# One PSUM pool of double banks for everything, longer score runs, and the first k loaded in three parts

## The chip, the cores and the metric

The kernel runs on one core of a Trainium2 chip. The metric is device time in microseconds (us) of that core. A span in a profile is counted from the first to the last instruction and is about 1.7 us shorter than the device time of the same run. Engines: PE is TensorE, PEld its weight loads, ACT is ScalarE, DVE is VectorE, POOL is GpSimd, SP is SyncE.

## The reference

Block-sparse attention (4 batches, 8 heads, 768 tokens, head size 64), then a two-layer network with a gated first layer. All in fp32.

```python
scores = q @ k.T / 8                       # 768 x 768 for each of 32 heads
scores = where(mask, scores, -1e9)         # window, first and last blocks, 3 random blocks a row
attn   = softmax(scores) @ v
x   = attn reordered to [3072 tokens, 512]
h   = x @ w_in                             # [3072, 2048]
g   = h * sigmoid(beta * h)
out = g @ w_out                            # [3072, 512]
```

## The kernel before

The kernel has a planner of its own. It describes all work as nodes with a planned duration and buffers, `order_of` puts the nodes in an order for each engine, and the instructions are emitted in that order. The buffers come from pools; the planner gives a buffer to a node when the slot is free by its own clock. The semaphore waits of the program come from the tiles that the instructions read and write, not from the planner.

PSUM holds two kinds of tiles: two double tiles of two banks each for scores (`sc`), four single banks for everything else (`mm`).

```python
SLOTS = {"st_k": 3, "st_q": 6, "st_v": 4, ..., "et": 15, "xst": 7, ..., "osb": 2,
         "sc": 2, "mm": 4}
...
T = {
    "sc": many(psum, "sc", [P, 2, 512], FP32),
    "mm": many(psum, "mm", [P, 512], FP32),
    ...
}
def at(buf):
    return T[buf.pool][buf.slot]
```

A score step fills one double tile (for two heads: 128 keys by 512 queries, or 256 by 256), and one exponential reads it whole:

```python
def mm(sc=sc, kc0=kc0):                       # "sc": 64 rows, the rest of PE's work has 128
    for i in range(kn):
        for hh in range(2):
            nc.tensor.matmul(at(sc)[:, hh, i * n:(i + 1) * n], lhsT=kX[...], rhs=qX[...],
                             start=True, stop=True)
def ex(eng, sc=sc, et=et):
    nc.scalar.activation(out=at(et)..., in_=at(sc)..., func=AF.Exp, bias=0.0, scale=SCALE)
```

The first layer makes 16 groups (`hp`) for each block of tokens; a tanh (`th`) on ACT and a gate multiply (`gm`) on DVE both read the group's bank. After them come the second-layer groups (`op`), whose bank is copied out to `osb`.

```python
for f in range(N_FFC):                        # 16
    hb, tb = Buf("mm"), Buf("t_sb")
    def hp(f=f, hb=hb):
        for c in range(NPAIR):                # 4
            nc.tensor.matmul(at(hb)[:, 0:n], lhsT=w_in_sb[:, c, f * P:(f + 1) * P],
                             rhs=xT_sb[:, c, t0:t0 + n], start=(c == 0), stop=(c == NPAIR - 1))
    def th(eng, f=f, hb=hb, tb=tb):
        nc.scalar.activation(out=at(tb)[:, 0:n], in_=at(hb)[:, 0:n], func=AF.Tanh,
                             bias=0.0, scale=beta_h_sb[:, f:f + 1])
    def gm(eng, f=f, hb=hb, tb=tb):
        nc.vector.scalar_tensor_tensor(out=at(gb)[:, f, 0:n], in0=at(tb)[:, 0:n], scalar=1.0,
                                       in1=at(hb)[:, 0:n], op0=ALU.add, op1=ALU.mult)
```

The rest of PE's work: transposes (`turn`, `xt`), attention times v (`av`, normalized by a reciprocal `rc` and a multiply `nm` on DVE). There are two token blocks of 256 (the first and the last) and five of 512.

The softmax here doesn't subtract the row's maximum and nothing guards it: scores larger than these inputs give would overflow.

Of the kernel before, what the change touches and what calls it, by code (L numbers as in the profile page):

```python
# [23 lines left out]
class Node:  # L24


    def __init__(self, kind, eng, dur, lat, emit, deps=(), take=(), use=(), moved=0,
# [10 lines left out]
        self.start = self.done = self.on = None  # L38


BIAS = {"av": 39, "beta": 625, "cast": 183, "dma": -860, "ex": 395, "gm": -151, "hp": 34,
        "load": 1245, "lone sc": 160, "mask": -541, "mk": 266, "next sc": -48, "norm": 134,
        "op": 45, "op on": 85, "osb": 304, "sc": -79, "spread": 28, "th": 302, "turn": -1220,
        "turn cp": 47, "weights": 444, "x cp": 29, "x turn": -13}

W_GATE = (3, "k")
SLACK = 1500.0
AHEAD = 3
HOP = 60.0
SWITCH = 100.0  # L50
RATE = {"SP": 305.0, "POOL": 410.0}
# [2 lines left out]
SHARED = 42.0  # L54


def order_of(nodes, free, slots):

    free = dict(free)
    give = {p: [(0.0, s) for s in range(n)] for p, n in slots.items()}  # L60
    rows = 128
    wire = {"SP": 0.0, "POOL": 0.0}
    port = {"DVE": 0.0, "POOL": 0.0}
    left, after, at_dep = {}, {}, {}
    todo = []
    for n in nodes:
        left[n] = len(n.deps)
        at_dep[n] = n.at
        for d, x in n.deps:
            after.setdefault(d, []).append((n, x))  # L70
        if not n.deps:
            todo.append(n)
    out = []
    while todo:
        best = None
        for n in todo:
            ready = at_dep[n]
            want = {}
            for b in n.take:
                want[b.pool] = want.get(b.pool, 0) + 1  # L80
            ok = True
            for p, c in want.items():
                if len(give[p]) < c:
                    ok = False
                    break
                ready = max(ready, sorted(give[p])[c - 1][0])
            if not ok:
                continue
            for e in n.eng:
                n_start = max(ready, free[e])  # L90
                if n.port and e in port:
                    n_start = max(n_start, port["POOL" if e == "DVE" else "DVE"])
                bias = BIAS[n.kind]
                if n.rows == 64:
                    if rows == 64:
                        bias += BIAS["next sc"]
                    elif sum(t <= n_start for t, _ in give["sc"]) < 2:
                        bias += BIAS["lone sc"]
                key = (n_start + n.dur[e] - min(n.dur.values()) + bias, n.place)
                if best is None or key < best[0]:  # L100
                    best = (key, n, e, n_start)
        if best is None:
            raise RuntimeError("no node can start")
        _, n, e, start = best
        if e == "PE" and n.rows != rows:
            start, rows = start + SWITCH, n.rows
        n.on, n.start = e, start
        free[e] = start + n.dur[e]
        if n.port and e in port:
            port[e] = free[e]  # L110
        if n.moved:
            other = "POOL" if e == "SP" else "SP"
            t, rest, rate = max(wire[e], start + DMA_FIRST[e]), n.moved, RATE[e]
            if e == "SP" and wire[other] > t:
                both = min(rest, (wire[other] - t) * SHARED)
                wire[other] += both / RATE[other]
                t, rest = t + both / SHARED, rest - both
            wire[e] = t + rest / rate
            n.done = wire[e] + DMA_LAST
        else:  # L120
            n.done = free[e] + n.tail
        for b in n.take:
            t, b.slot = min(give[b.pool])
            give[b.pool].remove((t, b.slot))
        for b in n.use:
            b.users -= 1
            b.end = max(b.end, n.done)
            if b.users == 0:
                give[b.pool].append((b.end + HOP, b.slot))
        todo.remove(n)  # L130
        out.append(n)
        for m, x in after.get(n, ()):
            at_dep[m] = max(at_dep[m], n.done + HOP + x)
            left[m] -= 1
            if left[m] == 0:
                todo.append(m)
    if len(out) < len(nodes):
        raise RuntimeError("some nodes never become ready")
    return out
# [3 lines left out]
def kernel(  # L143
# [16 lines left out]
    P = 128  # L160
# [9 lines left out]
    VW = D + 2  # L170
    Q1 = 256

    SLOTS = {"st_k": 3, "st_q": 6, "st_v": 4, "s16_k": 4, "s16_q": 2, "set": 4, "va": 5,
             "et": 15, "xst": 7, "recip": 6, "t_sb": 5, "g": 2, "osb": 2, "sc": 2, "mm": 4}

    persist = ctx.enter_context(tc.tile_pool(name="persist", bufs=1))
    psum = ctx.enter_context(tc.tile_pool(name="psum", bufs=1, space=bass.MemoryType.PSUM))
# [1 line left out]
    def many(pool, tag, shape, dtype):  # L179
        return [pool.tile(shape, dtype, name=f"{tag}_{i}") for i in range(SLOTS[tag])]  # L180

    T = {
        "sc": many(psum, "sc", [P, 2, 512], FP32),
        "mm": many(psum, "mm", [P, 512], FP32),
        "et": many(persist, "et", [P, 2, 512], FP16),
        "xst": many(persist, "xst", [P, 4, 2, D], FP16),
        "recip": many(persist, "recip", [P, 2, 2, 1], FP32),
# [10 lines left out]
        T[f"s16_{nm}"] = many(persist, f"s16_{nm}", [P, 2 * NC * D], FP16)  # L198

    def at(buf):  # L200
        return T[buf.pool][buf.slot]

    identity = persist.tile([P, P], FP16, name="identity")
# [157 lines left out]
    def by_chunk(s16, lo, hi):  # L361
        return at(s16)[:, lo * P:hi * P].rearrange("p (c h d) -> p h c d", h=2, d=D)

    def add_load(nm, x, st, lo, hi, gate):
        b, j = pairs[x]
        src = {"k": k, "q": q, "v": v}[nm]

        def load():
            hg = src[b, 2 * j:2 * j + 2].rearrange("h (g p c) d -> p (h g) (c d)", g=NG, p=P)
            o = at(st).rearrange("p h (g c) -> p (h g) c", g=NG)  # L370
            if hi - lo == NC:
                nc.sync.dma_start(out=o, in_=hg)
            else:
                for g in range(lo // CG, hi // CG):
                    nc.sync.dma_start(out=o[:, g::NG], in_=hg[:, g::NG])
        deps = [(d, -1e9) for d in last_load + begin]
        kw = {"take": [st]}
        if gate is not None:
            def shut():
                nc.gpsimd.tensor_copy(out=at(st)[0:1, 0, lo * D:lo * D + 1],  # L380
                                      in_=w_out_sb[0:1, gate * 8, 0:1])
            deps.append(add("weights", "POOL", 600, 50, shut, deps=[w_out_of[gate]], take=[st]))
            kw = {"use": [st]}
        last_load[:] = [add("load", "SP", 500 if hi - lo in (NC, CG) else 1000, 0, load, deps=deps,
                             moved=68000 * (hi - lo) + (500000 if x == 0 and nm == "v" else 0),
                             **kw)]
        return last_load[0]

    def add_cast(x, nm, st, dst, lo, hi, load):
        w = (hi - lo) * P  # L390

        def cast(eng):
            e = nc.vector.tensor_copy if eng == "DVE" else nc.gpsimd.tensor_copy
            src = at(st)[:, :, lo * D:hi * D].rearrange("p h (c d) -> p h c d", d=D)
            e(out=at(dst)[:, :, :, 0:D] if nm == "v" else by_chunk(dst, lo, hi),  # L395
              in_=src)
        return add("cast", ("DVE", "POOL"), {"DVE": 60 + 0.53 * w, "POOL": 50 + 0.94 * w}, 90, cast,
                   deps=[(load, SLACK if x >= NPAIR else 4000 if lo and x == 3 else 0)],
                   take=[dst], use=[st], port=True)

    def add_half(x, nm, kq, lo, hi, first, gate):

        i = "kq".index(nm)
        w = (hi - lo) * P
        st, s16 = Buf(f"st_{nm}"), Buf(f"s16_{nm}")
        load = add_load(nm, x, st, lo, hi, gate)
        if x < NPAIR and lo == 0:
            loads[x, nm] = st, load
        c = add_cast(x, nm, st, s16, lo, hi, load)
        if x >= N_PE_TURN:  # L410
            def turn():
                nc.sync.dma_start_transpose(
# [18 lines left out]
    def add_prep(x, gates=(None, None, None)):  # L431
        kq, va, st = Buf("set"), Buf("va"), Buf("st_v")
        hi = Q1 // P if x < NPAIR else NC
        tk = add_half(x, "k", kq, 0, NC, None, gates[0])
        tq = add_half(x, "q", kq, 0, hi, tk, gates[1])
        lv = add_load("v", x, st, 0, NC, gates[2])
        cv = add_cast(x, "v", st, va, 0, NC, lv)
        prep[x] = {"kq": kq, "va": va, "k": tk, "q": tq, "q on": tq, "v": cv}
        if x < NPAIR:
            loads[x, "v"] = st, lv  # L440

# [6 lines left out]
    def tile_steps(x, q0, n):  # L448
# [5 lines left out]
        for kc0 in range(0, NC, kn):  # L454
# [19 lines left out]
            def mk(eng, et=et, kc0=kc0):  # L474
# [3 lines left out]
                    [P, 2 * CG * kn, w])  # L478
                nc.vector.tensor_tensor(out=e, in0=e, in1=m, op=ALU.mult)  # L479

            steps.append((x, q0, sc, et, mm, ex, mk,
                          [mask_of[g] for g in range(q0 // (CG * P), (q0 + n) // (CG * P))]))
        return steps, ets

    sc_of = {}

    def add_step(step, unit):
        x, q0, sc, et, mm, ex, mk, masks = step
        r = prep[x]
        g = add("sc", "PE", 218, 180, mm, deps=[(r["k"], SLACK if x >= N_PE_TURN else 0),  # L490
                      (r["q"] if q0 == 0 else r["q on"], SLACK if x >= N_PE_TURN else 0)],
                take=[sc], use=[r["kq"]], rows=64)
        sc_of.setdefault(unit, g)
# [197 lines left out]
```

## Time and profile before

| | before |
|---|---|
| device time, median of 3 runs | 280.38 us (280.29 to 280.6) |
| profiled span | 280.1 us |
| busy share PE / ACT / DVE | 95% / 76% / 75% |
| the chain that ended last | 83% PE |

The profiled execution is one of its own, at 281.79 us. Its PE clock was 0.74 of full speed between 20 and 33 us and full before and after that up to 62 us.

From the page of the kernel before: its first part (busy us, share of the span), two rows of the 40 slices, the chain, and four groups of instructions (busy us, mean ns of one, idle time before them and what ended most of it):

```profile
PE 265.3 (95%) x2455; PEld 139.5 (50%) x2455; DVE 209.5 (75%) x424; ACT 212.9 (76%) x281; POOL 28.0 (10%) x45
...
PE   4597899999999999999999999999999999999994
...
PE 83%; ACT 7%; DVE 4%; DMA 3%; issue 2%; SPq 0%; ACTq 0%; DVEq 0%
...
L591 PE MATMUL mm<-w_out_sb,g 128*128 128x512 f16 x384 | 93.3, 380 | 0.0
L567 PE MATMUL mm<-xT_sb,w_in_sb 128*128 128x512 f16 (+1 forms) x448 | 89.9, 349 | 0.4
L576 DVE SCALAR_TENSOR_TENSOR g<-t_sb,mm 128x512 f16<-128x512 f16 (+1 forms) x112 | 66.0, 608 | 23.3 <-ACT t_sb L572 22.2
L572 ACT ACTIVATE t_sb<-mm,beta_h_sb 128x512 f16<-128x512 f32 (+1 forms) x112 | 67.8, 649 | 12.9 <-PE mm L567 12.1
```

L567 is the first layer, L591 the second; PE waits for nothing ahead of them (0.4 and 0.0 us in all). After the first eighth of the span PE is full, so in that part time falls only if PE gets less to do, and rises with any wait put in front of PE.

What the two readers of a bank do during a run of first-layer groups shows in the timeline of before at 231 us (start, duration, engine, instruction, number merged, idle before and releaser):

```profile
231.48 8.80 PE L567 MATMUL mm<-xT_sb,w_in_sb 128*128 128x512 f16 x40
...
234.13 0.69 DVE L576 SCALAR_TENSOR_TENSOR g<-t_sb,mm 128x512 f16<-128x512 f16 x1 [0.17 <-ACT t_sb L572]
234.27 0.69 ACT L572 ACTIVATE t_sb<-mm,beta_h_sb 128x512 f16<-128x512 f32 x1 [0.18 <-PE mm L567]
234.99 0.69 DVE L576 SCALAR_TENSOR_TENSOR g<-t_sb,mm 128x512 f16<-128x512 f16 x1 [0.17 <-ACT t_sb L572]
235.14 0.69 ACT L572 ACTIVATE t_sb<-mm,beta_h_sb 128x512 f16<-128x512 f32 x1 [0.18 <-PE mm L567]
```

PE runs on without a gap. A group of four matmuls takes about 0.86 us; a tanh and a multiply take 0.69 us each, and the tanh of one group runs beside the multiply of the group ahead. Both wait for PE, not PE for them.

The gain that the change is after shows in the chain of waits of before (start, duration, what):

```profile
159.58 0.54 PE sc L462 x4
160.12 0.97 PE mm L567 x4
161.09 0.86 PE mm L591 x4
```

Two score steps take 0.54 us to the next start, where streaming alone is 0.43 us, and a four-matmul group at the edge of a score run takes 0.97 us instead of 0.86. So each run of score steps costs 0.11 us on each side, 0.21 us in all: score steps use 64 rows of the array, all else 128. The Trainium skill states a reason ("TensorEngine Tiling (Array Packing)", Key Properties: a change of the tiling mode drains the TensorEngine); it gives no number, this trace does. The trace shows the cost and not its reason.

### The profile page before, as it was taken

To read this page: it belongs to the slowest core of one execution; us is meant where nothing else is said; L and a number is where in the kernel's file an instruction comes from. 1 tells how busy PE (TensorE), PEld (TensorE's weight loads), DVE (VectorE), ACT (ScalarE), POOL (GpSimd) and SP (SyncE) were. 2 spreads that over 40 slices of the span, in tenths; PEclk is the share of its full clock that TensorE was granted. 3 is DMA by queue.
4 is the path that set the end of the run, shared out by engine and by line. 5 is a ranking of instruction groups with operands and counts; after the bars stand their busy time and mean duration, and the time that the engine had idled before them with its cause. 6 is when DMAs were issued, how large, how long until landed. Compare 5 with 4: busy or idle time off the path is not lost.

```text
span 280.1 us, 6128 instructions
## 1 busy us (share of the span) xinstructions
PE 265.3 (95%) x2455; PEld 139.5 (50%) x2455; DVE 209.5 (75%) x424; ACT 212.9 (76%) x281; POOL 28.0 (10%) x45
## 2 busy tenths in 40 slices
PE   4597899999999999999999999999999999999994
PEld 1364576654363664454563354643355554556741
DVE  5697999999995788887789998877876787733500
ACT  1689898879987898997879988879966877704611
POOL 5560010010200010231001310010000000000000
PEclk9997799999999999999999999999999999999999
DMA  7999994899602194996227986860102010011112
GB/s 204 292 251 213 202 176 115 109 305 233 163 4 37 48 247 115 303 252 150 68 70 204 266 207 86 248 104 35 39 2 77 37 49 37 0 22 75 40 55 96
DMA packets 72849, 36.65 MB, mean 131 GB/s; under 512 B 29796, under 2 KB 68724, under 8 KB 72820
## 3 DMA queue, kind: packets, MB, share of 16 engines
q1 hardware_dynamic: 69568, 32.06, 47.0%
q0 software_dynamic: 3136, 4.19, 8.6%
q8 instruction: 19, 0.31, 0.5%
q14 instruction: 10, 0.08, 0.1%
q10 hardware_dynamic: 116, 0.01, 0.0%
HBM read 27.27 MB, written 6.29 MB: 120 GB/s over the span
## 4 chain that ended last, share of the span: by engine, by line
PE 83%; ACT 7%; DVE 4%; DMA 3%; issue 2%; SPq 0%; ACTq 0%; DVEq 0%
PE mm L591 29%; PE mm L567 28%; PE mm L517 12%; PE sc L462 12%; ACT et L470 5%; DMA st_k<-in_k_dram 2%; PE mm L420 1%; DMA sb_i<-in_sampled_blocks_dram 1%; DVE g L576 1%; DVE et L479 1%; ACT t_sb L572 1%; DVE s_k L395 1%; ACT qX L425 0%; DVE s_q L395 0%; ACT kX L425 0%
## 5 line engine op out<-in xcount | busy, mean ns | idle before, releaser
L470 ACT ACTIVATE et<-sc 128x1024 f16<-128x1024 f32 x144 | 142.2, 1031 | 24.7 <-PE sc L462 22.0
L479 DVE TENSOR_TENSOR et<-et,mask 128x1024 f16<-128x1024 f16 x144 | 98.6, 695 | 20.0 <-ACT et L470 19.7
L591 PE MATMUL mm<-w_out_sb,g 128*128 128x512 f16 x384 | 93.3, 380 | 0.0
L567 PE MATMUL mm<-xT_sb,w_in_sb 128*128 128x512 f16 (+1 forms) x448 | 89.9, 349 | 0.4
L576 DVE SCALAR_TENSOR_TENSOR g<-t_sb,mm 128x512 f16<-128x512 f16 (+1 forms) x112 | 66.0, 608 | 23.3 <-ACT t_sb L572 22.2
L572 ACT ACTIVATE t_sb<-mm,beta_h_sb 128x512 f16<-128x512 f32 (+1 forms) x112 | 67.8, 649 | 12.9 <-PE mm L567 12.1
L567 PEld LDWEIGHTS <-w_in_sb 128*128 128x128 f16 x448 | 42.4, 98 | 44.5 <-issue 6.8
L591 PEld LDWEIGHTS <-g 128*128 128x128 f16 x384 | 33.7, 98 | 43.6 <-issue 11.5
L462 PE MATMUL sc<-qX,kX 64*128 64x256 f16 (+1 forms) x384 | 48.4, 342 | 4.3 <-ACT et L470 3.0
L517 PEld LDWEIGHTS <-et 128*128 128x128 f16 x1152 | 42.3, 100 | 9.2 <-issue 3.1
L517 PE MATMUL mm<-va,et 128*128 128x65 f16 x1152 | 44.5, 196 | 0.0
L462 PEld LDWEIGHTS <-kX 64*128 64x128 f16 x384 | 15.5, 96 | 26.9 <-issue 21.8
L601 ACT ACTIVATE osb<-mm 128x512 f32<-128x512 f32 x16 | 9.6, 599 | 18.9 <-PE mm L591 18.7
L527 DVE TENSOR_TENSOR xst<-mm,recip 128x256 f16<-128x256 f32 x48 | 20.1, 419 | 0.4
L395 POOL CAST s_q<-st_q 128x768 f16<-128x768 f32 (+1 forms) x10 | 8.5, 847 | 92.8 <-DMA st_q<-in_q_dram 89.5
L524 DVE RECIPROCAL recip<-mm 128x4 f32<-128x4 f32 x48 | 8.5, 178 | 5.5 <-PE mm L517 4.9
L395 POOL CAST va<-st_v 128x768 f16<-128x768 f32 x7 | 6.9, 983 | 15.4 <-DMA st_v<-in_v_dram 15.4
L395 DVE CAST s_k<-st_k 128x768 f16<-128x768 f32 x12 | 7.9, 656 | 0.7 <-DMA st_k<-in_k_dram 0.7
L395 DVE CAST va<-st_v 128x768 f16<-128x768 f32 x9 | 4.9, 546 | 1.5 <-DMA st_v<-in_v_dram 1.5
L395 POOL CAST s_k<-st_k 128x768 f16<-128x768 f32 x4 | 3.5, 875 | 20.8 <-DMA st_k<-in_k_dram 20.8
L603 DVE TENSOR_SCALAR osb<-mm 128x512 f32<-128x512 f32 x8 | 5.5, 684 | 0.0
L395 DVE CAST s_q<-st_q 128x512 f16<-128x512 f32 (+2 forms) x10 | 4.5, 454 | 0.0
(53 smaller groups left out, 44.3 us busy)
## 6 DMA issues: line engine op xcount, KB each, us to landing
st_k<-in_k_dram SPq DMA_DIRECT2D x16, 384.0 KB, 4.8
st_v<-in_v_dram SPq DMA_DIRECT2D x16, 384.0 KB, 5.3
out_dram<-osb SPq DMA_DIRECT2D x24, 256.0 KB, 2.0
st_q<-in_q_dram SPq DMA_DIRECT2D x12, 384.0 KB, 4.6
w_in_sb<-in_moe_w_in_dram POOLq DMA_DIRECT2D x2, 1024.0 KB, 12.0
w_out_sb<-in_moe_w_out_dram POOLq DMA_DIRECT2D x2, 1024.0 KB, 21.2
st_q<-in_q_dram SPq DMA_DIRECT2D x12, 128.0 KB, 4.6
xT_sb<-xst SPq DMA_TRANSPOSE x22, 2.4
```

What stands on the lines that cost most here:

```text
L395: e(out=at(dst)[:, :, :, 0:D] if nm == "v" else by_chunk(dst, lo, hi), in_=src)
L462: nc.tensor.matmul(at(sc)[:, hh, i * n:(i + 1) * n], lhsT=kX[hh * D:(hh + 1) * D, (kc0 + i) * P:(kc0 + i + 1) * P], rhs=qX[hh * D:(hh + 1) ...
L470: nc.scalar.activation(out=at(et).rearrange("p h q -> p (h q)"), in_=at(sc).rearrange("p h q -> p (h q)"), func=AF.Exp, bias=0.0, scale=SCALE)
L479: nc.vector.tensor_tensor(out=e, in0=e, in1=m, op=ALU.mult)
L517: nc.tensor.matmul(a[:, i, hh, :], lhsT=at(ets[kc // kn])[:, hh, at0:at0 + P], rhs=at(va)[:, hh, kc, 0:D + 1], start=(kc == 0), stop=(kc = ...
L524: nc.vector.reciprocal(out=at(rb), in_=av_ap()[:, :, :, D:D + 1])
L527: nc.vector.tensor_tensor(out=at(xs)[:, half * 2:half * 2 + 2], in0=av_ap()[:, :, :, 0:D], in1=at(rb).to_broadcast([P, 2, 2, D]), op=ALU.mult)
L567: nc.tensor.matmul(at(hb)[:, 0:n], lhsT=w_in_sb[:, c, f * P:(f + 1) * P], rhs=xT_sb[:, c, t0:t0 + n], start=(c == 0), stop=(c == NPAIR - 1))
L572: nc.scalar.activation(out=at(tb)[:, 0:n], in_=at(hb)[:, 0:n], func=AF.Tanh, bias=0.0, scale=beta_h_sb[:, f:f + 1])
L576: nc.vector.scalar_tensor_tensor(out=at(gb)[:, f, 0:n], in0=at(tb)[:, 0:n], scalar=1.0, in1=at(hb)[:, 0:n], op0=ALU.add, op1=ALU.mult)
L591: nc.tensor.matmul(at(ob), lhsT=at(gb)[:, f, ts * P:(ts + 1) * P], rhs=w_out_sb[:, f, :], start=(f == 0), stop=(f == N_FFC - 1))
L601: nc.scalar.activation(out=at(sb), in_=at(ob), func=AF.Copy, bias=0.0, scale=0.5)
```

## The change

Its intent: fewer switches of mode. Eight banks are now four double tiles, so that up to three score steps can stand in a row, and every other PE result takes one half of a double tile. The planner keeps its books bank by bank (`bank[2*d]`, `bank[2*d+1]`), with a limit on how many tiles each kind may hold. The k of pair 0 is loaded, cast and turned in three parts, so that the first score needs only one of them. Bias values of the planner and some SBUF buffer counts were tuned anew.

```diff
+IN_PARTS = (0,)
+BANKS = ("sc", "mm")
+MOST = {"av": 8, "hp": 6, "sc": 3}
+def banks_of(b):
+    return (2 * b.slot, 2 * b.slot + 1) if b.pool == "sc" else (b.slot,)
...
+def bank_for(bank, pool, t):
+    if pool == "sc":
+        ok = [d for d in range(len(bank) // 2) if whole(bank, d, t)]
+        return min(ok, key=lambda d: max(bank[2 * d:2 * d + 2]))
+    ok = [i for i in range(len(bank)) if bank[i] is not None and bank[i] <= t]
+    def other(i):
+        return float("inf") if bank[i ^ 1] is None else bank[i ^ 1]
+    return max(ok, key=lambda i: (other(i), -i))
...
-    SLOTS = {"st_k": 3, "st_q": 6, "st_v": 4, "s16_k": 4, "s16_q": 2, "set": 4, "va": 5,
-             "et": 15, "xst": 7, "recip": 6, "t_sb": 5, "g": 2, "osb": 2, "sc": 2, "mm": 4}
+    SLOTS = {"st_k": 2, "st_q": 5, "st_v": 5, "s16_k": 4, "s16_q": 2, "set": 4, "va": 4,
+             "et": 13, "xst": 5, "recip": 7, "t_sb": 6, "g": 2, "osb": 3, "sc": 4}
...
         "sc": many(psum, "sc", [P, 2, 512], FP32),
-        "mm": many(psum, "mm", [P, 512], FP32),
...
     def at(buf):
+        if buf.pool == "mm":
+            return T["sc"][buf.slot // 2][:, buf.slot % 2]
         return T[buf.pool][buf.slot]
...
-        tk = add_half(x, "k", kq, 0, NC, None, gates[0])
-        tq = add_half(x, "q", kq, 0, hi, tk, gates[1])
+        if x in IN_PARTS:
+            work = Buf("st_k"), Buf("s16_k")
+            for g in range(NG):
+                parts.append(add_half(x, "k", kq, g * CG, g * CG + CG,
+                                      parts[0] if parts else None, None, work))
+                if g == 0:
+                    tq = add_half(x, "q", kq, 0, hi, parts[0], None)
...
(cut: the new BIAS table, the planner's bank bookkeeping, a score step's dependence on its part of k)
```

More of the change, by code (lines that the diff above doesn't have):

```diff
@@ L38, in __init__ @@
         self.start = self.done = self.on = None
-BIAS = {"av": 39, "beta": 625, "cast": 183, "dma": -860, "ex": 395, "gm": -151, "hp": 34,
-        "load": 1245, "lone sc": 160, "mask": -541, "mk": 266, "next sc": -48, "norm": 134,
-        "op": 45, "op on": 85, "osb": 304, "sc": -79, "spread": 28, "th": 302, "turn": -1220,
-        "turn cp": 47, "weights": 444, "x cp": 29, "x turn": -13}
+BIAS = {"av": -69, "beta": -455, "cast": 94, "dma": -1239, "ex": 257, "gm": -727, "hp": -468,
+        "load": 1496, "lone sc": 331, "mask": -1415, "mk": 241, "next sc": 94, "norm": -152,
+        "op": -13, "op on": -70, "osb": 284, "sc": -204, "spread": -316, "th": 422,
+        "turn": -3422, "turn cp": -88, "two sc": -72, "weights": 774, "x cp": -31,
+        "x turn": -102}
 W_GATE = (3, "k")
@@ L54, with whole, soonest @@
 SHARED = 42.0
+BANKS = ("sc", "mm")
+MOST = {"av": 8, "hp": 6, "sc": 3}
+def banks_of(b):
+    return (2 * b.slot, 2 * b.slot + 1) if b.pool == "sc" else (b.slot,)
+def whole(bank, d, t):
+    return all(x is not None and x <= t for x in bank[2 * d:2 * d + 2])
+def soonest(bank, pool):
+    if pool == "mm":
+        return min((t for t in bank if t is not None), default=None)
+    pairs = [bank[i:i + 2] for i in range(0, len(bank), 2)]
+    return min((max(p) for p in pairs if None not in p), default=None)
+def bank_for(bank, pool, t):
[6 more added lines that the diff above has]
+    return max(ok, key=lambda i: (other(i), -i))
 def order_of(nodes, free, slots):
     free = dict(free)
-    give = {p: [(0.0, s) for s in range(n)] for p, n in slots.items()}
+    give = {p: [(0.0, s) for s in range(n)] for p, n in slots.items() if p not in BANKS}
+    bank, held = [0.0] * (2 * slots["sc"]), {}
     rows = 128
@@ L81, in order_of @@
             ok = True
+            if held.get(n.kind, 0) >= MOST.get(n.kind, 99):
+                continue
             for p, c in want.items():
+                if p in BANKS:
+                    t = soonest(bank, p)
+                    if t is None:
+                        ok = False
+                        break
+                    ready = max(ready, t)
+                    continue
                 if len(give[p]) < c:
@@ L96, in order_of @@
                         bias += BIAS["next sc"]
-                    elif sum(t <= n_start for t, _ in give["sc"]) < 2:
-                        bias += BIAS["lone sc"]
+                    else:
+                        room = sum(whole(bank, d, n_start) for d in range(len(bank) // 2))
+                        bias += BIAS["lone sc"] if room < 2 else BIAS["two sc"] if room < 3 else 0
                 key = (n_start + n.dur[e] - min(n.dur.values()) + bias, n.place)
@@ L122, in order_of @@
         for b in n.take:
+            if b.pool in BANKS:
+                b.slot, b.kind = bank_for(bank, b.pool, start), n.kind
+                held[n.kind] = held.get(n.kind, 0) + 1
+                for i in banks_of(b):
+                    bank[i] = None
+                continue
             t, b.slot = min(give[b.pool])
@@ L127, in order_of @@
             b.end = max(b.end, n.done)
-            if b.users == 0:
+            if b.users == 0 and b.pool in BANKS:
+                held[b.kind] -= 1
+                for i in banks_of(b):
+                    bank[i] = b.end + HOP
+            elif b.users == 0:
                 give[b.pool].append((b.end + HOP, b.slot))
@@ L362, in by_chunk, with add_load @@
         return at(s16)[:, lo * P:hi * P].rearrange("p (c h d) -> p h c d", h=2, d=D)
-    def add_load(nm, x, st, lo, hi, gate):
+    def add_load(nm, x, st, lo, hi, gate, more=False):
         b, j = pairs[x]
@@ L376, in add_load @@
         deps = [(d, -1e9) for d in last_load + begin]
-        kw = {"take": [st]}
+        kw = {"use" if more else "take": [st]}
         if gate is not None:
@@ L384, in add_load, with add_cast @@
         last_load[:] = [add("load", "SP", 500 if hi - lo in (NC, CG) else 1000, 0, load, deps=deps,
-                             moved=68000 * (hi - lo) + (500000 if x == 0 and nm == "v" else 0),
+                             moved=68000 * (hi - lo) + (170000 if x == 0 and nm == "v" else 0),
                              **kw)]
         return last_load[0]
-    def add_cast(x, nm, st, dst, lo, hi, load):
+    def add_cast(x, nm, st, dst, lo, hi, load, more=False):
         w = (hi - lo) * P
@@ L398, in add_cast, with add_half @@
                    deps=[(load, SLACK if x >= NPAIR else 4000 if lo and x == 3 else 0)],
-                   take=[dst], use=[st], port=True)
-    def add_half(x, nm, kq, lo, hi, first, gate):
+                   take=[] if more else [dst], use=[st] + ([dst] if more else []), port=True)
+    def add_half(x, nm, kq, lo, hi, first, gate, at_work=None):
         i = "kq".index(nm)
         w = (hi - lo) * P
-        st, s16 = Buf(f"st_{nm}"), Buf(f"s16_{nm}")
-        load = add_load(nm, x, st, lo, hi, gate)
+        st, s16 = at_work or (Buf(f"st_{nm}"), Buf(f"s16_{nm}"))
+        load = add_load(nm, x, st, lo, hi, gate, at_work and lo > 0)
         if x < NPAIR and lo == 0:
             loads[x, nm] = st, load
-        c = add_cast(x, nm, st, s16, lo, hi, load)
+        c = add_cast(x, nm, st, s16, lo, hi, load, at_work and lo > 0)
         if x >= N_PE_TURN:
@@ L433, in add_prep @@
         hi = Q1 // P if x < NPAIR else NC
-        tk = add_half(x, "k", kq, 0, NC, None, gates[0])
-        tq = add_half(x, "q", kq, 0, hi, tk, gates[1])
+        parts = []
+        if x in IN_PARTS:
[5 more added lines that the diff above has]
+                    tq = add_half(x, "q", kq, 0, hi, parts[0], None)
+            tk = parts[0]
+        else:
+            tk = add_half(x, "k", kq, 0, NC, None, gates[0])
+            tq = add_half(x, "q", kq, 0, hi, tk, gates[1])
         lv = add_load("v", x, st, 0, NC, gates[2])
         cv = add_cast(x, "v", st, va, 0, NC, lv)
-        prep[x] = {"kq": kq, "va": va, "k": tk, "q": tq, "q on": tq, "v": cv}
+        prep[x] = {"kq": kq, "va": va, "k": tk, "q": tq, "q on": tq, "v": cv,
+                   "k of": parts or [tk] * NG}
         if x < NPAIR:
@@ L479, in mk @@
                 nc.vector.tensor_tensor(out=e, in0=e, in1=m, op=ALU.mult)
-            steps.append((x, q0, sc, et, mm, ex, mk,
+            k_of = prep[x]["k of"][kc0 // CG:(kc0 + kn - 1) // CG + 1]
+            steps.append((x, q0, k_of, sc, et, mm, ex, mk,
                           [mask_of[g] for g in range(q0 // (CG * P), (q0 + n) // (CG * P))]))
@@ L487, in add_step @@
     def add_step(step, unit):
-        x, q0, sc, et, mm, ex, mk, masks = step
+        x, q0, k_of, sc, et, mm, ex, mk, masks = step
         r = prep[x]
-        g = add("sc", "PE", 218, 180, mm, deps=[(r["k"], SLACK if x >= N_PE_TURN else 0),
+        g = add("sc", "PE", 218, 180, mm, deps=[(t, SLACK if x >= N_PE_TURN else 0)
+                                           for t in dict.fromkeys(k_of)] + [
                       (r["q"] if q0 == 0 else r["q on"], SLACK if x >= N_PE_TURN else 0)],
```

## The prediction

> **What bounds the kernel now.** The page's first part has TensorE (PE) busy 265.3 of 280.1 us (95%), ScalarE 212.9, VectorE 209.5; the chain of waits is 83% PE. Busy time by stretches: until 33 us PE has gaps (data, exponentials), from 47 to 270 us almost none, so there every us of PE work or wait counts.
>
> **What the change removes.** In the built program's order on PE, score matmuls (64 rows) stand in 78 runs before and 55 after (34 of three steps). In the chain, a run of two steps takes 0.54 us to the next start where streaming is 0.43, and the 128-row group at its edge 0.97 instead of 0.86: 0.21 us per run. The Trainium skill agrees ("TensorEngine Tiling (Array Packing)", Key Properties: changing the tiling mode drains the array). 23 runs are worth 4.8 us, 16 of them (3.4 us) in the PE-bound part. k of pair 0 in three parts: first scores start at 8.12 us now; PE still stands behind the mask chain (6.0 us), so I give it 1 us. Taken alone: about 275 us.
>
> **What it adds.** All non-score matmuls now use halves of the four double tiles, and the built program tracks a double tile as one thing. Its waits show it: of 112 tanh, some 47 wait for the PE group that fills the *other* half, 41 for VectorE's gate multiply on the other half, and 29 first-layer (hp) groups for that multiply. The planner in the kernel doesn't know these waits; nothing like it stood before. (The skill's "PSUM — Partial Sum Buffer" lets ScalarE and VectorE work in parallel on different banks; these waits are the program's, not the chip's.) The order also puts all 16 hp groups of a token block in one row, and in the first two 512 blocks they alternate over two doubles only.
>
> Cost of a pair, with durations of the before trace at 231 to 240 us: two hp groups 1.73, then tanh, multiply, tanh, multiply one behind the other at 0.72 each (0.69 busy + hop) and 0.05 to PE: 4.65 us until the double can be filled again. With two doubles that is 4.65 us per four groups instead of 3.45. My estimates: first two 512 blocks +6 us each (4 in the row, 2 at its end), the other three +3 to +5, the two 256 blocks +4 each. At the end, second-layer (op) groups alternate over the halves of one double and wait for the copy of the other half: five times 0.7 = 3.5 us. In the second-layer stretches some 25 waits of av, op and score groups for norms and copies of the other half, 0.3 to 0.7 us each. Together +35 to +45; some overlaps with waits on ScalarE that exist anyway: I take +34.
>
> **Prediction: 309 us**, 8 in 10 between 294 and 322. Faster by over 2%: 0.05; within 2%: 0.05; slower: 0.90.
>
> **What would show it.** PE busy share well under 95%, its idle put down to VectorE's multiply, norm and ScalarE's copy. Rows of 16 hp groups: 17 to 19 us per 512 block instead of 13.8, ScalarE and VectorE taking turns. PE work itself about 5 us less. First scores near 7 us. Gaps of 0.7 us in the final second-layer stretch.
>
> **What would make it wrong.** If most of these waits are met before PE needs them, 276 to 285. If idle PE is granted a lower clock (0.74 between 20 and 33 us now), slower than 322.

## The result, and the profile after

| | before | after |
|---|---|---|
| device time, median | 280.34 us (279.56 to 280.6, 4 runs) | 336.65 us (335.79 to 337.45, 4 runs) |
| ratio | | 1.2014 (95% interval 1.1974 to 1.2054) |
| profiled span, mean clock of PE | 280.1 us, 0.988 | 334.1 us, 0.985 |

A ratio here and below is the mean time of one kernel's runs over that of the other's in the same rounds, so not quite the ratio of the medians quoted.

The changed kernel is 20% slower. The direction was predicted, the size was not: 309 us predicted, outside the range at 336.65.

From the page of the changed kernel, the lines that answer to those of before (L637 is the first layer, L642 the tanh, L646 the gate multiply, L661 the second layer):

```profile
PE 273.9 (82%) x2455; PEld 143.1 (43%) x2455; DVE 207.3 (62%) x416; ACT 216.5 (65%) x284; POOL 31.5 (9%) x53
...
PE   6777768877779898887999989896889898887884
...
PE 59%; DVE 21%; ACT 14%; issue 3%; DMA 1%; ACTq 0%; DVEq 0%
...
L637 PE MATMUL sc<-xT_sb,w_in_sb 128*128 128x512 f16 (+1 forms) x448 | 90.0, 348 | 20.5 <-DVE g L646 18.9
L642 ACT ACTIVATE t_sb<-sc,beta_h_sb 128x512 f16<-128x512 f32 (+1 forms) x112 | 66.6, 624 | 54.8 <-PE sc L637 30.8
L661 PE MATMUL sc<-w_out_sb,g 128*128 128x512 f16 x384 | 91.7, 379 | 11.6 <-DVE xst L597 6.1
...
L646 DVE SCALAR_TENSOR_TENSOR g<-t_sb,sc 128x512 f16<-128x512 f16 (+1 forms) x112 | 66.0, 610 | 51.4 <-ACT t_sb L642 50.9
```

No instruction became slower: the means of the four groups hardly moved. What is new is the idle time in front of them. PE had none before its two large groups and now has 20.5 and 11.6 us; ACT and DVE idle beside it (54.8 and 51.4 us, where it was 12.9 and 23.3). In the chain, DVE and ACT together went from 11% to 35%. All three engines are less busy in share, and none took over as the limit: this is the picture of engines that take turns. PE's busy time even rose from 265.3 to 273.9 us although its matmuls are the same 2455 with fewer mode switches. The Trainium skill warns against reading it as progress ("Perfetto Trace Analysis", Identifying the Most-Contended Engine: matmul busy time is not a good measure of nearness to roofline), and this trace agrees: 8.6 us more busy time is no more work.

The same stage as shown for before, a row of first-layer groups, in the timeline of the changed kernel at 130 us:

```profile
130.02 0.69 ACT L642 ACTIVATE t_sb<-sc,beta_h_sb 128x512 f16<-128x512 f32 x1 [0.55 <-PE sc L637]
130.25 1.89 PE L637 MATMUL sc<-xT_sb,w_in_sb 128*128 128x512 f16 x8 [0.26 <-DVE g L646]
...
130.74 0.69 DVE L646 SCALAR_TENSOR_TENSOR g<-t_sb,sc 128x512 f16<-128x512 f16 x1 [0.55 <-ACT t_sb L642]
...
131.46 1.39 ACT L642 ACTIVATE t_sb<-sc,beta_h_sb 128x512 f16<-128x512 f32 x2 [0.75 <-DVE g L646]
132.18 1.39 DVE L646 SCALAR_TENSOR_TENSOR g<-t_sb,sc 128x512 f16<-128x512 f16 x2 [0.76 <-ACT t_sb L642]
132.92 1.89 PE L637 MATMUL sc<-xT_sb,w_in_sb 128*128 128x512 f16 x8 [0.79 <-DVE g L646]
...
135.07 1.89 PE L637 MATMUL sc<-xT_sb,w_in_sb 128*128 128x512 f16 x8 [0.26 <-DVE g L646]
```

The tanh waits for a *multiply* (0.75 us) and PE waits for a multiply (0.79 us) where before a tanh waited only for PE. Nothing in the mathematics makes a tanh wait for the multiply of another group. The two groups only lie in the two halves of one double tile. Four groups take 4.82 us (130.25 to 135.07) instead of 3.45.

The built program says the same. Of 112 tanh, 47 carry a wait for the PE group that fills the other half and 41 one for the multiply that reads the other half; 29 first-layer groups wait for a multiply on the other half. Counting all waits between two instructions that share no bank, or that both only read it, and no other written data, the changed program has 277 and the one before 20. (A recount on the programs built again gave 279 and 20. Of the 279, 248 are between different halves of a double tile; these are the *other-half waits* below. The 31 others, and all 20 of before, are between two readers of one bank.)

The summary of waits of the changed kernel, PE alone (us in total, times, longest):

```profile
PE sc L637 <- DVE g L646: 18.9, 34, 1.2
PE sc L661 <- DVE xst L597: 6.1, 9, 0.9
PE sc L587 <- DVE g L646: 3.7, 4, 1.7
PE sc L661 <- ACT osb L671: 3.5, 5, 0.7
PE sc L587 <- DVE osb L673: 3.1, 4, 0.8
```

Not one of these kinds is in the same summary of before, whose largest was 3.0 us (scores waiting for an exponential). A second-layer group (L661) has no reason in the data to wait for a norm of attention (L597) or for the copy of another token tile (L671), unless it takes over the same bank. In the built program all 12 of its waits for a norm and 6 of its 7 for a copy are for the other half.

### The profile page after: what moved, and what is told of

Read it like the earlier page. It is cut to its first block, busy times and chain, and to the rows that moved or that the text cites. A ratio compares the mean times of both kernels' runs of the same rounds, so it can differ in the third digit from the quotient of the medians.

```text
span 334.1 us, 6124 instructions
## 1 busy us (share of the span) xinstructions
PE 273.9 (82%) x2455; PEld 143.1 (43%) x2455; DVE 207.3 (62%) x416; ACT 216.5 (65%) x284; POOL 31.5 (9%) x53
## 4 chain that ended last, share of the span: by engine, by line
PE 59%; DVE 21%; ACT 14%; issue 3%; DMA 1%; ACTq 0%; DVEq 0%
PE sc L661 25%; PE sc L637 14%; PE sc L587 11%; DVE g L646 11%; ACT t_sb L642 10%; PE sc L530 7%; DVE xst L597 3%; DVE et L547 3%; ACT et L538 2%; ACT osb L671 2%; DVE recip L594 1%; PE sc L477 1%; DVE osb L673 1%; DMA sb_i<-in_sampled_blocks_dram 1%; DVE xT_sb L615 1%
## 5 line engine op out<-in xcount | busy, mean ns | idle before, releaser
L637 PE MATMUL sc<-xT_sb,w_in_sb 128*128 128x512 f16 (+1 forms) x448 | 90.0, 348 | 20.5 <-DVE g L646 18.9
L642 ACT ACTIVATE t_sb<-sc,beta_h_sb 128x512 f16<-128x512 f32 (+1 forms) x112 | 66.6, 624 | 54.8 <-PE sc L637 30.8
L661 PE MATMUL sc<-w_out_sb,g 128*128 128x512 f16 x384 | 91.7, 379 | 11.6 <-DVE xst L597 6.1
L646 DVE SCALAR_TENSOR_TENSOR g<-t_sb,sc 128x512 f16<-128x512 f16 (+1 forms) x112 | 66.0, 610 | 51.4 <-ACT t_sb L642 50.9
L637 PEld LDWEIGHTS <-w_in_sb 128*128 128x128 f16 x448 | 43.6, 97 | 66.2 <-issue 30.3
L661 PEld LDWEIGHTS <-g 128*128 128x128 f16 x384 | 35.1, 97 | 56.8 <-issue 22.3
L587 PE MATMUL sc<-va,et 128*128 128x65 f16 x1152 | 44.6, 197 | 11.8 <-DVE g L646 3.7
L671 ACT ACTIVATE osb<-sc 128x512 f32<-128x512 f32 x18 | 10.7, 597 | 27.4 <-PE sc L661 18.1
L594 DVE RECIPROCAL recip<-sc 128x4 f32<-128x4 f32 x48 | 8.6, 179 | 28.0 <-PE sc L587 9.6
L597 DVE TENSOR_TENSOR xst<-sc,recip 128x256 f16<-128x256 f32 x48 | 20.4, 424 | 1.8 <-DVE recip L594 0.2
L452 POOL CAST s_k<-st_k 128x768 f16<-128x768 f32 (+1 forms) x11 | 8.2, 743 | 100.8 <-DMA st_k<-in_k_dram 100.8
L452 POOL CAST s_q<-st_q 128x768 f16<-128x768 f32 (+2 forms) x11 | 9.1, 826 | 40.5 <-DMA st_q<-in_q_dram 38.7
```

Of the source, the lines that this page charges most:

```text
L452: e(out=at(dst)[:, :, :, 0:D] if nm == "v" else by_chunk(dst, lo, hi), in_=src)
L587: nc.tensor.matmul(a[:, i, hh, :], lhsT=at(ets[kc // kn])[:, hh, at0:at0 + P], rhs=at(va)[:, hh, kc, 0:D + 1], start=(kc == 0), stop=(kc = ...
L594: nc.vector.reciprocal(out=at(rb), in_=av_ap()[:, :, :, D:D + 1])
L597: nc.vector.tensor_tensor(out=at(xs)[:, half * 2:half * 2 + 2], in0=av_ap()[:, :, :, 0:D], in1=at(rb).to_broadcast([P, 2, 2, D]), op=ALU.mult)
L661: nc.tensor.matmul(at(ob), lhsT=at(gb)[:, f, ts * P:(ts + 1) * P], rhs=w_out_sb[:, f, :], start=(f == 0), stop=(f == N_FFC - 1))
L671: nc.scalar.activation(out=at(sb), in_=at(ob), func=AF.Copy, bias=0.0, scale=0.5)
```

## The experiments

All kernels below gave correct results. In the diffs, x is the later instruction and y the earlier one; `declare_no_dep` takes the dependence between two instructions out of the program. It is only used where the two are on different engines, their banks of the double tile are disjoint, and they share no other tensor that one of them writes, so no wait is taken that the data needs.

**Theory:** the order on the engines is fine; the other-half waits are the whole loss. **Rivals:** the tuned order or the smaller SBUF pools lose the time (then it stays without those waits); or two engines in the two banks of one double tile are slow on the chip itself (then it stays too).

### All other-half waits taken out, same order (e1_by_bank, repeated as e11_by_bank_again)

```diff
+def by_bank(tc):
+    near = {}
+    for block in tc.nc.m.functions[0].blocks:
+        for x in block.instructions:
+            psum, other = touched(x)         # banks of double tiles; all other tensors, r or w
+            for name, banks, side in psum:
+                past = near.setdefault(name, [])
+                for y, y_banks, y_other in past:
+                    if y.engine == x.engine or y_banks & banks:
+                        continue
+                    if not any(n in y_other and "w" in (other[n], y_other[n]) for n in other):
+                        tc.declare_no_dep(x, y, reason="other bank")
+                past.append((x, banks, other))
... (cut: a counter, and a limit of 200 on the length of past)
     with tc.manual_schedule():
         ...emit in the planner's order
+        by_bank(tc)
```

> The changed kernel with the same order on every engine and the same banks; only the waits between instructions that touch different halves of a double tile are taken away (the two halves are two PSUM banks and share no data, so no race). Theory (waits for the other half cost everything): PE work falls by the 23 score runs and nothing is given back, so 272 to 280 us, with rows of 16 first-layer groups at 13.8 to 14.5 us per 512 block. Rival 1 (the order itself is bad: 16 groups in a row starve ScalarE's exponentials, three score steps fill PSUM): stays above 300 us. Rival 2 (a mixture): 285 to 300.

Measured: 277.54 us (276.7 to 277.87), 0.9874 of before (0.9847 to 0.9902), where before had 281.04 us in the same rounds. The repeat, in five rounds on another chip:

> The same kernel as in the first experiment (all waits for the other half freed, same order), once more in five rounds and perhaps on another chip: 276.5 to 278.5 us, 0.98 to 0.995 of the kernel before, if the first result holds; nearer to 1 if it was luck of the start.

It gave 277.6 us (276.56 to 278.5), 0.9895 (0.9871 to 0.9918), with before at 280.68. The order on all engines is that of the changed kernel; the count of waits without shared data falls from 277 to 51. By the recount none of the 248 other-half waits is left, and all 51 are between two readers of one bank.

Both rivals fall. The order and the pools cost nothing against before, and two engines at work in the two halves of a double tile at once neither slow each other in these traces nor give wrong results. Here is a row of first-layer groups again, now without the waits:

```profile
107.62 0.69 DVE L685 SCALAR_TENSOR_TENSOR g<-t_sb,sc 128x512 f16<-128x512 f16 x1 [0.17 <-ACT t_sb L681]
107.77 0.69 ACT L681 ACTIVATE t_sb<-sc,beta_h_sb 128x512 f16<-128x512 f32 x1 [0.18 <-PE sc L676]
```

The tanh waits for PE alone and runs beside the multiply of the group ahead, both in 0.69 us, as before the change; by the built program these two read the two halves of one double tile. The Trainium skill agrees that they may ("PSUM — Partial Sum Buffer", Specifications and Summary: ScalarE and VectorE run in parallel at full bandwidth if their banks differ, and PSUM is to be guarded by bank). One row of 512 tokens and the stretch behind it, and the last second-layer stretch, in both kernels (window, its length, then busy us of PE, PEld, DVE, ACT, POOL, granted clock of PE, DMA share, GB/s). The changed kernel:

```profile
127.20:145.80 18.60, 15.06 (x66) 6.12 (x65) 10.79 (x16) 10.99 (x16) 2.48 (x3) 1.00 0.86 215
145.80:177.60 31.80, 28.29 (x355) 15.73 (x355) 24.33 (x52) 25.92 (x30) 1.65 (x2) 1.00 0.50 115
307.20:329.80 22.60, 19.08 (x86) 8.10 (x84) 1.21 (x3) 4.29 (x8) 0.00 (x0) 1.00 0.16 59
```

The same three stages without the other-half waits:

```profile
103.20:117.20 14.00, 14.00 (x67) 6.18 (x67) 11.09 (x17) 11.58 (x17) 2.48 (x3) 1.00 0.84 176
117.20:144.90 27.70, 27.54 (x356) 15.48 (x356) 25.04 (x52) 25.14 (x29) 1.86 (x2) 1.00 0.86 188
252.50:270.80 18.30, 18.26 (x86) 8.07 (x83) 1.06 (x3) 3.63 (x7) 0.00 (x0) 1.00 0.19 73
```

The work in each is the same to within an instruction or two at the window's edge, the clock is full in all; 4.6, 4.1 and 4.3 us are gone.

This gives a measure of where the loss lies. Both kernels have the same order on PE, so the span can be cut at the same instructions: at the first group of each row of 16 first-layer groups and after its last. Time from PE's instruction records, in us:

| stage | after | e1 | lost | e4 | e5 |
|---|---|---|---|---|---|
| first matmul to first row | 33.39 | 28.79 | 4.60 | 30.86 | 32.46 |
| the seven first-layer rows, sum | 109.48 | 83.55 | 25.93 | 110.00 | 83.38 |
| the six stretches between, sum | 163.08 | 138.87 | 24.21 | 143.17 | 160.12 |
| last second-layer stretch | 22.62 | 18.30 | 4.32 | 18.29 | 22.62 |
| sum | 328.57 | 269.51 | 59.06 | 302.32 | 298.58 |

(e4 and e5 are the next two experiments.)

### Which waits: those of the gated rows, or all others (e5_gate_rows_only, e4_rest_only)

The same function with one more condition. `gate_part` is true of the first-layer matmuls, the tanh and the multiply.

```diff
                     if y.engine == x.engine or y_banks & banks:
                         continue
+                    if not (gate_part(x) and gate_part(y)):   # e5: free only waits among these
+                    if gate_part(x) and gate_part(y):         # e4: free all other-half waits but these
+                        continue
```

> The complement of e3_tanh_rows_only: first-layer matmuls, tanh and multiply keep their waits for the other half among themselves, all other other-half waits (attention-value, norms, copies, scores, second layer) are freed. Without overlap: about 336.6 - 33 = 304 us (299 to 310). With overlap: 312 to 330.

Measured: 307.67 us (307.05 to 309.39), 1.0961 of before (1.092 to 1.1002).

> What e3 was meant to be (its edit freed nearly all waits, see the count of waits in the built programs): only waits among first-layer matmuls, tanh and gate multiply are freed from the other half, all others of the changed kernel stay. In the changed kernel the seven first-layer rows took 27 us over their work, the stretches between and the end 30. If the two groups of waits add up: 336.6 - 27 = 310 us (305 to 314), with rows at 13.8 to 14.2 us and the excess of the stretches kept. If the stretches lose time only because the rows before them leave ScalarE and VectorE behind: 280 to 295.

Measured: 305.17 us (303.41 to 305.85), 1.0842 (1.0781 to 1.0902).

By the recount e4 keeps 117 other-half waits, exactly the three kinds of the gated rows (47, 41 and 29), and e5 keeps none of these three. Each does in the table what it should: e4 leaves the rows (110.00) and clears the last stretch (18.29) and most of the stretches between; e5 clears the rows (83.38) and leaves the rest. What PE still waits for shows in the summaries of waits. With only the rest freed:

```profile
PE sc L685 <- DVE g L694: 18.2, 32, 1.2
```

And with only the gated rows freed:

```profile
PE sc L709 <- DVE xst L645: 5.7, 9, 0.9
PE sc L709 <- ACT osb L719: 3.5, 5, 0.7
PE sc L635 <- DVE osb L721: 3.1, 4, 0.8
```

The two gains, from the changed kernel's 336.65 us, are 29.0 and 31.5 us, 60.5 together; both at once (e1) gain 59.1. They add up, to within the spread of about 2 us of each kernel's runs: the two groups of waits do not hide each other. The prediction had allowed for an overlap with waits on ACT that exist anyway. No run tests that alone, but there was little to overlap with: between 47 and 266 us PE of before is busy for 218.65 of 219.00 us.

### A failed edit (e3_tanh_rows_only)

This was meant to be e5. The condition was written as below; in Python it reads `A and (B is not True)`, so it keeps only the waits of a gated instruction for another kind and frees nearly everything.

```diff
+                    if gate_part(x) and gate_part(y) is not True:
+                        continue
```

> As e1_by_bank, but only the waits among first-layer matmuls, tanh and gate multiply are freed from the other half; all others stay. Traces put 26 us of the excess into the rows of 16 first-layer groups, and about 29 into the stretches between and the end. If the parts add up without overlap: about 336.6 - 26 = 311 us (306 to 316). If the waits hide each other (my prediction discounted for that): much less than 26 gained, 318 to 330.

Measured: 278.92 us (277.79 to 280.5), 0.9932 (0.989 to 0.9975). It tests nothing of what was expected. The built program explains it: 54 waits without shared data are left against 51 in e1 (by the recount, 7 other-half waits of 248). It only repeats e1's verdict, and is told because the number alone would have looked like proof that the gated rows are the whole loss, which e5 then refuted.

### Which wait within the gated rows (e8_tanh_after_gate, e9_tanh_after_hp, e10_hp_after_gate)

One kind of wait freed at a time, again in the changed kernel's order:

```diff
+                    if (part(x), part(y)) != ("th", "gm"):                        # e8: 41 waits
+                    if (part(x), part(y)) not in (("th", "hp"), ("gm", "hp")):    # e9: 47 waits
+                    if (part(x), part(y)) != ("hp", "gm"):                        # e10: 29 waits
+                        continue
```

(In e9 the multiply had to be freed too: with the tanh alone freed, the built program moves the wait for the other half's fill to the multiply behind it.)

> Of all other-half waits only the 41 of tanh for VectorE's multiply on the other half (a read that waits for a read) are freed. Chain of a pair then: two groups 1.73, 0.04, two tanh at 0.60 to 0.65, then the second multiply 0.69, 0.05: about 3.9 us per double in place of 4.65. Rows of the first two 512 blocks (two doubles): 15.3 to 16 us in place of 18.5; the other three rows (three doubles) 14 to 15. Total 319 to 326. Rival (these waits are met anyway, the refill waits alone count): above 331.

> The changed kernel in its own order; freed are only the 47 waits of a tanh, and of the gate multiply behind it, for the first-layer group that fills the other half. Theory (the half tiles of a double go round one ring: fill, fill, tanh, multiply, tanh, multiply, 4.65 us): the ring loses one fill, 0.86 us, so 3.8 us where two doubles take turns; rows of 512 tokens at 18.5 come to 15 to 16, total 321 to 327 us. Rival (the waits are redundant with each other, so that freeing one kind only moves the waiting to the next): rows keep 17.5 or more and the total stays over 331. The stretches between the rows and the last one keep their extra time in both.

> The changed kernel in its own order; freed are only the 29 waits of a first-layer group for the gate multiply that reads the other half. Theory of the ring: the first half can be filled one tanh and one multiply earlier, but its tanh still waits for the second fill, which waits for the second multiply: the ring also loses about one fill (0.86 us), rows at 18.5 come to 15 to 16, total 321 to 327 us. Rival (redundant waits): rows keep 17.5 or more, total over 331.

Measured: e8 323.65 us (322.62 to 326.15), 1.1522 (1.1451 to 1.1592); e9 315.3 us (314.72 to 317.35), 1.1249 (1.1216 to 1.1283); e10 330.38 us (328.79 to 332.96), 1.1782 (1.1735 to 1.183). The rows, us each (rows 1 and 7 are the blocks of 256 tokens):

| row | after | e8 | e9 | e10 | e1 |
|---|---|---|---|---|---|
| 1 | 12.48 | 10.82 | 9.20 | 12.42 | 7.22 |
| 2 | 18.46 | 17.18 | 17.34 | 15.97 | 13.90 |
| 3 | 18.57 | 15.92 | 16.57 | 15.67 | 13.91 |
| 4 | 15.31 | 13.91 | 14.62 | 14.22 | 13.91 |
| 5 | 17.90 | 17.79 | 13.82 | 17.90 | 13.81 |
| 6 | 15.75 | 15.13 | 13.81 | 15.22 | 13.81 |
| 7 | 11.01 | 10.82 | 7.50 | 10.95 | 6.99 |

The total met its expectation in e8; in e9 it came out lower than expected, and in e10 between the theory and its rival. Part of the totals of e8 and e10 is not the freed wait: their profiled starts took 30.94 and 30.80 us against 33.39, at a higher clock (see the end of the next section). The rows are the test, and they say where the theory failed: it had one ring for all rows, and the program has at least two.

- Rows 2 and 3 fill a, b of one double, then a, b of another. Fill, fill, tanh, multiply, tanh, multiply go round, and each of the three kinds of wait is a link. Freeing any one shortens rows 2 and 3 by 1.1 to 2.9 us. Not all came to the 15 to 16 us expected: row 2 stayed at 17.18 in e8 and 17.34 in e9, row 3 at 16.57 in e9. The traces say where the rest went. In the middle of these rows four groups take 4.82 to 4.89 us in the changed kernel, 3.99 us in e8 (3.9 expected) and 4.20 us in e9 (3.8 expected). Row 2 also spent 7.39 (e8) and 7.12 us (e9) on its first six groups. Why e9 is slower than its ring, and row 2 slow to start, was not tested.
- In row 5 the built program hands one double back and forth: the tanh of a group in half a waits for the *next* fill of half b, that fill for the multiply that empties half b, and that multiply's tanh for the fill of half a. A fill, a tanh and a multiply follow each other for every two groups. The wait for the fill is a link of it, the other two kinds are not. So e9 clears row 5 to 13.82, and e8 (expected to shorten it) and e10 leave it at 17.79 and 17.90.

### Parts of the change alone (e2_parts_alone, e6_by_bank_no_parts, e7_by_bank_two_in_row)

These let the planner lay a new order, so each changes the order as well as the named part.

```diff
e2: the kernel before
+IN_PARTS = (0,)        # with the code of the change for loading, casting and turning k in three
e6: e1
-IN_PARTS = (0,)
+IN_PARTS = ()
e7: e1
-MOST = {"av": 8, "hp": 6, "sc": 3}
+MOST = {"av": 8, "hp": 6, "sc": 2}
```

> The kernel before with one part of the change alone: k of pair 0 loaded, cast and turned in three parts (the planner lays a new order for it, with the old biases and pools). Theory: the parts have nothing to do with the loss: 279 to 282 us, first scores 0.5 to 1.3 us earlier than 8.1. Rival (the parts delay the other loads): above 285.

> e1_by_bank without the three parts of k of pair 0 (the planner lays a new order: 57 score runs, one row of 16 split in two). Theory: the parts are worth about 1 us at the start: 277 to 280. Rival after e2 (the parts cost time): 274 to 276.5.

> e1_by_bank with at most two score steps at once held in PSUM (68 score runs in place of 55, of which some are still of three). At 0.21 us per run the 13 more cost 2.7 us of TensorE work: 279.5 to 281.5. Rival (runs cost nothing, the pool alone gains): 277 to 278.5.

Measured: e2 283.32 us (281.77 to 284.13), 1.0066 (1.0027 to 1.0106); e6 281.62 us (281.41 to 282.12), 1.0019 (0.9965 to 1.0072); e7 285.42 us (284.81 to 285.95), 1.0149 (1.0102 to 1.0195).

All three missed. The parts bring nothing when put into the old kernel (it even loses 0.7%, though its first scores start at 6.39 us instead of 8.12); taking them out of e1 costs 4.1 us; allowing two score steps instead of three costs 7.9 us. The prediction's 0.21 us for each run of score steps covers 2.7 us of the last: e7 has 68 runs against 55. The rest was not taken apart. The bias values were tuned for the whole change, so these three say that the pieces belong together with that tuning, and not what each is worth.

## Why the prediction was wrong in size and right in direction

**Right: what bounds it, and what the cost is made of.** PE was the limit, and the other-half waits of the built program are the loss: e1 shows that they are all of it, but for some 2 us at the start that may be the clock (below). Most signs named came true: in rows 2 and 3 the pairs go round two doubles as described, at 4.82 us for four groups where 4.65 was predicted; PE busy at 82%, its idle time put down to the multiply, the norm and the copies; gaps of 0.68 and 0.69 us in the last stretch, as here in the changed kernel:

```profile
309.79 3.61 PE L661 MATMUL sc<-w_out_sb,g 128*128 128x512 f16 x16 [0.68 <-ACT osb L671]
...
313.44 0.60 ACT L671 ACTIVATE osb<-sc 128x512 f32<-128x512 f32 x1 [3.70 <-PE sc L661]
314.09 3.61 PE L661 MATMUL sc<-w_out_sb,g 128*128 128x512 f16 x16 [0.69 <-ACT osb L671]
```

Two signs failed in part: only three of the five rows of 512 tokens fell in 17 to 19 us (rows 4 and 6 took 15.31 and 15.75), and PE's own busy time, which was to fall by 5 us, rose by 8.6.

**Nearly right: the change without these waits.** Predicted "about 275 us", measured 277.5 (e1). PE's busy time there is 259.5 us, 5.8 us less than before, where about 5 us was predicted; part of the difference may be the clock, which was 0.74 at 20 to 33 us in the profile of before and 1.00 in that of e1.

**Right in sum, partly by luck: the rows; nearly right: the last stretch.** Predicted for the rows themselves about 28 us (4 us in each of the first two 512 blocks, 3 to 5 in the other three, 4 in each 256 block: 8 + 12 + 8), measured 25.93. In single rows the spread is larger, and the errors cancel: rows 4 and 6 lost 1.40 and 1.94, row 1 lost 5.26, and row 5 lost its 4.09 by a ring that the prediction did not have (see above). The last stretch: 3.5 predicted, 4.32 measured.

**Wrong, the step that failed: the sum of the wait costs, and the discount on it.** The items as the text lists them come to 40 to 56 us: 12 for the first two 512 blocks, 9 to 15 for the other three, 8 for the two 256 blocks, 3.5 at the end, and 7.5 to 17.5 for the 25 waits. The text wrote "+35 to +45", and then took 34, because "some overlaps with waits on ScalarE that exist anyway". So 48, the middle of its own items, became 34. The runs show 59.1 us: e4 and e5 gain 29.0 and 31.5 us, and 59.1 together, so the waits do not hide each other. PE had next to no idle time in which to hide them either (before, 0.35 us between 47 and 266 us).

The miss of 27.65 us is made up so: 14 from the cut of 48 to 34; 11 from the items themselves (stretches between the rows 7.7 too small, the start 4.6, the last stretch 0.8, less 2.1 for the rows); 2.5 because the kernel without these waits takes 277.5 us and not 275. Even the upper end of the items, 275 + 56 = 331 us, would have been too low.

**Mis-sized: the stretches between the rows.** The estimate was some 25 waits of 0.3 to 0.7 us, so 7.5 to 17.5 us, and 4 us more at the ends of rows 2 and 3, 16.5 in the middle. Measured: 24.21 us. The text counted the waits that PE itself holds. The program also makes ACT and DVE wait for other halves: 13 reciprocals and 13 copies of the second layer for an av group, 10 such copies for a norm, and more. What they then finish late may be what PE waits for under a different name; no run frees these alone, so their share is not shown. e4 frees them together with PE's own, and 19.9 of the 24.21 us come back (163.08 to 143.17).

**Mis-sized: the start.** A gain of 1 us was predicted. The first scores did start earlier, 6.79 against 8.12 us, as these two lines of the timeline of PE show. Before:

```profile
8.12 1.03 PE L462 MATMUL sc<-qX,kX 64*128 64x256 f16 x8 [0.66 <-ACT qX L425]
```

After:

```profile
6.79 1.46 PE L530 MATMUL sc<-qX,kX 64*128 64x256 f16 x12
```

But up to the first row the changed kernel takes 4.60 us more than e1. How much of that is the waits is not shown, because the clock differs too: PE's granted clock from 20 to 33 us was 0.66 in the changed kernel's profile, 1.00 in e1 and its repeat. The starts of the profiled runs (the first row of the stage table), by that clock:

| clock at 20 to 33 us | waits of the start kept | waits of the start freed |
|---|---|---|
| 1.00 | 30.94 (e8), 30.80 (e10) | 28.79 (e1), 28.49 (its repeat), 30.35 (e3) |
| 0.63 to 0.74 | 33.39 (after, 0.66), 33.32 (e9, 0.67), 32.46 (e5, 0.74) | 30.86 (e4, 0.63) |

In this table the lower clock goes with 0.5 to 2.5 us, and the waits, at the full clock, with 0.4 to 2.5 us. Neither is sharper, because the start also differs between runs for another reason: e3, which by the recount has no other-half wait before its first row, took 1.56 us more than e1 at the same clock (at 8 to 11 us PE stood idle for 2.88 us, behind a cast of k; in e1 for 1.17 us). What sets the clock is open: before also had 0.74 there, and the prediction named this risk. It is of the order of 1%, and no explanation of the 56 us: the mean clock was 0.985 in all four runs of the changed kernel, and 0.988 in the profile of before.

**Open:** what the parts of k and the third score step are each worth in one fixed order; why rows 2 and 3 did not shorten further in e8 and e9; what the waits of the start are worth apart from the clock; how much of the stretches is due to waits of ACT and DVE; what sets the clock at 20 to 33 us.

**The version that beats both** is e1: 277.5 us, 1.0 to 1.3% under before and 17.6% under the changed kernel (277.54 over 336.65), in two series on two chips. Against before both intervals lie clear of 1.

## What to carry to other kernels

When two buffers become halves of one tile, look at the waits of the built program and not only at the planner's books: the planner here kept accounts by bank, the program's waits went by whole tile, and 59 us lay between the two. Count the new waits on every engine, not just on the one that limits, add the items up as they stand, and give no discount for overlap where the trace shows no idle time of the limiting engine to hide them in. Remedies are to free waits between disjoint banks, where that can be shown safe, or to keep separate tiles for what is not used together (the kernel before does so, and has no other-half wait).

## What the Trainium skill lacked or had wrong

- "TensorEngine Tiling (Array Packing)", Key Properties, says that a change of mode drains the array, and gives no cost. Here a run of 64-row score matmuls among 128-row ones costs 0.21 us: 0.54 us for two steps that stream in 0.43 us, and 0.97 instead of 0.86 us for the group at its edge.
- "PSUM — Partial Sum Buffer", Summary, says to guard by bank. It doesn't say what a coarser guard costs. Here waits by double tile cost 59.1 us of 336.65, and with them removed two engines worked in two banks of one tile with correct results.
- "Perfetto Trace Analysis", Optimization Strategy, says that the same gap repeating on the engine that should be full can mean too little room for the next tile. Here the gap of 0.79 us repeats, and the cause was the grain of the waits: with the same eight banks and the same order (e1) it was gone.
- I found no point of these pages that a run contradicted.
